# An attention and GLU block on one core: one PSUM sum for the first two head groups, its bank given to the scores, and a reshaped end

## Chip, cores, metric

The kernel runs on one core of a Trainium2 chip. The metric is the device time of one execution in microseconds (us), the median of several executions.

## The reference

One transformer block on 2048 tokens of width 640, in bf16: 32 heads of 20 columns, then a gated feed-forward part of width 1728 without a non-linearity.

```python
def reference(A_x, A_wqkv, A_wo, B_x, B_w_gate, B_w_up, B_w_down):
    def _A_ref(x, wqkv, wo):            # x: 1 x 2048 x 640, 32 heads of Dh = 20
        ...                             # q, k, v from x @ wqkv
        scores = jnp.einsum("bhqd,bhkd->bhqk", q, k) * (Dh ** -0.5)
        p = _softmax(scores, axis=-1)
        o = jnp.einsum("bhqk,bhkd->bhqd", p, v)
        return o...reshape(B, S, D) @ wo
    def _B_ref(x, w_gate, w_up, w_down):
        return ((x @ w_gate) * (x @ w_up)) @ w_down      # einsums in the original
    h = x + _A_ref(_layernorm(x), A_wqkv, A_wo)
    return h + _B_ref(_layernorm(h), B_w_gate, B_w_up, B_w_down)
```

## The kernel before

Names that the text uses. The queries are cut into six pieces p of 512, 512, 384, 256, 256 and 128; heads come in eight groups g of four. A *bank* is one 128 x 512 tile of scores (keys by queries); there are 2048, and the text tells the position in the kernel by them. Scores of a burst go to A0 or A1 in PSUM; ScalarE turns a burst into E = exp(scores) in one instruction; some banks go to VectorE instead, which computes the exponential with int16 arithmetic ("i", "fr", "hl", "ED" tiles). TensorE multiplies E with V into the bank `acc` (the row of ones in V gives the softmax sum as well). Everything else of TensorE (projections, Wo, gate, up, down) is *background work* in the banks `m`, and a scheduler in the build decides the order of all instructions from estimated durations: the order is fixed when the kernel runs. Once attention is over, the score banks become five more banks `b` for background work.

PSUM and the first two groups, which alternate by chunk of keys while K and V are still being made:

```python
acc = psum.tile([P, QW], F32, name="acc", tag="acc")
mb = tiles(psum, 2, [P, QW], F32, "m")
A = [None, pools[0].tile([P, 2, QW], F32, name="A1", tag="A1")]
A[0] = early.tile([P, 2, QW], F32, name="A0", tag="A0")
acc2 = early.tile([P, QW], F32, name="acc2", tag="acc2")   # the sum of group 1
...
# later, when group 1 is summed (about bank 128): early.release(), A0 gets 3 banks
order = [[(g, 4 * c + i) for c in range(NCH) for g in range(2) for i in range(4)]] + order[2:]
```

Every background matmul with 128 output rows is issued as four, each with its own weight load:

```python
def columns(ps, lhsT, rhs, start, stop, n, width=P):
    for i in range((width + 31) // 32):
        w = min(32, width - 32 * i)
        mm(ps[32 * i:32 * i + w, 0:n], lhsT[:, 32 * i:32 * i + w], rhs, start, stop)
```

The quotients of a finished group, with three DMAs to spread the reciprocals over the partitions:

```python
def normalise(p, g, ev):
    free = en.add("DVE", ..., tensor_copy(a[:, 0:w], bank[:, 0:w]))
    e = dma(s_ <- a[DH:P:32, 0:w])                 # the sums, to 32 partitions a head
    e = en.add("DVE", ..., reciprocal(r_, s_))
    e = dma(d <- r_)                               # to DRAM
    e = dma(b <- d, each row to 32 partitions)
    e = en.add("DVE", ..., tensor_tensor(OnT[g], a, b, ALU.mult))
```

The first loads and who waits for them:

```python
e_qk0 = [None, load_w(D, D + 160)]
e_qk0[0] = load_w(0, 160)
...
ws = ([e_k, e_qk0[1]] if b == 1 else [e_q, e_qk0[0]]) if g == 1 else [e_qk0[b]]
```

The softmax here doesn't subtract the row's maximum and nothing guards it: scores larger than these inputs give would overflow.

Of the kernel before, what the change touches and what calls it, by code (L numbers as in the profile page):

```python
# [41 lines left out]
PADR = 12  # L42
WIDTHS = [512, 512, 384, 256, 256, 128]
LASTP = len(WIDTHS) - 1
TURNED = 0
RES = 5

# [141 lines left out]
class Pe:  # L189
# [54 lines left out]
    def bg_act(self, g):  # L244
        def act(s):
            dur, fn, deps = g.steps[g.at]
            deps = list(deps)
            if g.bank is None:
                self.groups.remove(g)
                self.opens.append(g)  # L250
                deps += g.deps
                g.bank = min((b for b in self.mbanks if b.free.t is not None), key=lambda b: b.free.t)
                deps.append(g.bank.free)
                g.bank.free = Ev()
            last = g.at == len(g.steps) - 1
            self.charge(s, dur, "C", dur * 2.4, deps, [g.ev] if last else [])
            fn(g.bank.ap, g.at == 0, g.at == len(g.steps) - 1)
            g.at += 1
            if last:
                self.opens.remove(g)  # L260
                g.bank.free = g.evac(g.bank.ap, g.ev)
        return act

    def next(self):
# [4 lines left out]
        if t < INF and (kind == 2 or s > t + 100.0):  # L269
            if known([self.zeros]) <= t and sum(w for x, w in self.recent if x > t - TICK) < ENOUGH:  # L270
                need = FILL + SWITCH + (SWITCH if self.mode != "C" else 0.0)
# [5 lines left out]
    def fill(self, s):  # L277
# [3 lines left out]
        if new:  # L281
            b = next((b for b in self.mbanks if b.free.t is not None and b.free.t <= s), None)
            if b is None:
                b = Bank(self.att.acc_of(1, 0))
                b.free = self.att.acc_free[0]
            bank, deps = b.ap, deps + [b.free]
        n = bank.shape[1]
        self.charge(s, n / 2.4 + 3.0, "C", float(n), deps, [])
# [39 lines left out]
SPREAD = 1.2  # L328
# [3 lines left out]
LAG = 100  # L332
# [3 lines left out]
def kernel(  # L336
# [27 lines left out]

    pools = [tc.alloc_tile_pool(name="second", bufs=1, space=PSUM)]
    A = [None, pools[0].tile([P, 2, QW], F32, name="A1", tag="A1")]
    early = tc.alloc_tile_pool(name="early", bufs=1, space=PSUM)
    A[0] = early.tile([P, 2, QW], F32, name="A0", tag="A0")
    acc2 = early.tile([P, QW], F32, name="acc2", tag="acc2")
    late = []  # L370

    def single_banks():
# [3 lines left out]
        late[0].release()  # L376
# [11 lines left out]
    kap4 = keep.tile([P, HP], F32, name="kap4")  # L388
    kT = tiles(keep, G, [P, S], BF16, "kT")
# [11 lines left out]
    r7s = tiles(keep, 2, [P, HP], F32, "r7_")  # L401
    o7s = tiles(keep, 2, [P, P], BF16, "o7_")
# [28 lines left out]
    def columns(ps, lhsT, rhs, start, stop, n, width=P):  # L431

        for i in range((width + 31) // 32):
# [31 lines left out]
    class Att:  # L465
        def __init__(self):
# [5 lines left out]
            for p, w in enumerate(WIDTHS):  # L472
                nb = NT * w // QW
                order = [[(g, kg) for kg in range(nb)] for g in range(G)]
                if p == 0:
                    order = [[(g, 4 * c + i) for c in range(NCH) for g in range(2) for i in range(4)]] + order[2:]
# [10 lines left out]
            self.sums = {key: v // HP for key, v in self.left.items()}  # L487
# [9 lines left out]
            self.unit = 0  # L497
            self.a_free = [Ev(0.0), Ev(0.0)]
# [6 lines left out]
            self.acc_free = [Ev(0.0), Ev(0.0)]  # L505
# [67 lines left out]
        def wants_d(self):  # L573
# [8 lines left out]
            return load < D_LOAD  # L582
# [36 lines left out]
        def summing(self):  # L619
# [3 lines left out]
            for s in self.pv_left:  # L623
                p, g, _ = self.slots[s]
                if (p, g) in self.begun and not self.transposed(p, g):
                    return self.acc_of(p, g)[:, 0:WIDTHS[p]]
            return None

        def between(self, t):
# [3 lines left out]
            p, g, _ = self.slots[self.pv_left[0]]  # L633
            return (p, g) not in self.begun and self.acc_free[0].t is not None and self.acc_free[0].t <= t

        def transposed(self, p, g):
            return p == LASTP and g >= G - TURNED

        def acc_of(self, p, g):
            return acc2[:] if (p, g) == (0, 1) else acc[:]  # L640

        def s_option(self, t):
# [5 lines left out]
            at = max(t, self.a_free[u].t)  # L648
            size = 3 - u
            if u == 0 and not late and (self.acc_free[1].t is None or self.pv_at == 0 or self.acc_free[1].t > at):  # L650
                size = 2
# [6 lines left out]
        def s_act(self, u, banks):  # L658
            def act(s):
                size = len(banks)  # L660
                if size == 3 and not late:
                    early.release()
                    late.append(tc.alloc_tile_pool(name="late", bufs=1, space=PSUM))
                    A[0] = late[0].tile([P, 3, QW], F32, name="A0", tag="A0")
# [3 lines left out]
                if self.wants_d():  # L668
                    fr = [b for b in pe.mbanks if b.free.t is not None and b.free.t <= s]
                    ok = fr and self.late() <= LAG  # L670
# [130 lines left out]
        def pv_option(self, t):  # L801
# [3 lines left out]
            for s in self.pv_left:  # L805
# [8 lines left out]
                if (p, g) not in self.begun:  # L814
# [3 lines left out]
                    deps.append(self.acc_free[1 if (p, g) == (0, 1) else 0])  # L818
                rt = max(t, known(deps))
                if rt < best[0]:  # L820
                    turned = self.transposed(p, g)
                    dur = len(todo) * HP * 66.0 if turned else sum(pe_ns(n) for _, _, n, _ in todo)
                    best = rt, self.pv_act(s, es, todo, deps, dur, turned), dur, "D" if turned else "C"
# [4 lines left out]
        def pv_act(self, s, es, todo, deps, dur, turned):  # L828
            p, g, kg = self.slots[s]
            a = 1 if (p, g) == (0, 1) else 0  # L830

            def act(start):
                pe.charge(start, dur, "D" if turned else "C", 0.0 if turned else dur * 2.4, deps, [self.pv_ev[s]])
                bank = self.acc_of(p, g)
                self.sums[p, g] -= 1
                first = (p, g) not in self.begun
                self.begun.add((p, g))
                for i, (k, q, n, c) in enumerate(todo):

                    opens = first and i == 0  # L840
                    ends = self.sums[p, g] == 0 and i == len(todo) - 1
                    for j in range(HP):
                        h = g * HP + j
                        if turned:
                            mm(bank[:, VS * j:VS * j + VS], es[j][0][:, c:c + n], Vx[:, k, h * VS:h * VS + VS], opens and j == 0, ends and j == HP - 1)
                        else:
                            mm(bank[32 * j:32 * j + 32, q:q + n], Vx[:, k, h * VS:h * VS + 32],
                               es[j][0][:, c:c + n], opens, ends)
# [3 lines left out]
                if self.sums[p, g] == 0:  # L852
                    if turned:
                        self.acc_free[a] = last_quotients(g, self.pv_ev[s])
                    else:
                        self.acc_free[a] = normalise(p, g, self.pv_ev[s])
                if not self.pv_left:
# [7 lines left out]
    def filler(bank, new):  # L865
        for i in range(HP):
            mm(bank[32 * i:32 * i + 32, :], zt[:, 0:32], zt[:, 0:bank.shape[1]], new, new)
# [13 lines left out]

    def normalise(p, g, ev):
# [11 lines left out]
        bank = att.acc_of(p, g)  # L894
        free = en.add("DVE", dve_ns(w), [ev] + was,
                      lambda: nc.vector.tensor_copy(a[:, 0:w], bank[:, 0:w]), 0.5)
# [19 lines left out]
        return free  # L916

# [21 lines left out]

    def last_quotients(g, ev):  # L940

        sums = acc[:, 0:HP * VS].rearrange("p (h e) -> p h e", e=VS)
        r7, o7 = r7s[g % 2], o7s[g % 2]
        e = en.add("DVE", 110.0, [ev], lambda: nc.vector.reciprocal(r7[:].rearrange("p (h o) -> p h o", o=1), sums[:, :, DH:VS]), 0)
        e = en.add("DVE", 150.0, [e, e_o7], lambda: nc.vector.tensor_tensor(
            o7[:].rearrange("p (h e) -> p h e", e=32)[:, :, 0:DH], sums[:, :, 0:DH],
            r7[:].rearrange("p (h o) -> p h o", o=1).to_broadcast([P, HP, DH]), ALU.mult), 0)

        def turn(ps, first, last):
            pt = ps.bitcast(BF16)  # L950
            for i in range(HP):
                nc.tensor.transpose(pt[32 * i:32 * i + 32, 0:P], o7[:, 32 * i:32 * i + 32], ident[:])

        def evac(ps, x):
            q = en.add("DVE", dve_ns(P), [x, Later(lambda: wo_done.get(LASTP - 1))], lambda: nc.vector.tensor_copy(OnT[g][:, 0:P], ps.bitcast(BF16)[:, 0:P]), 0)
            on_ev[LASTP, g] = q
            return q
        front = [x for x in pe.groups if g == G - 1 and x.tag[:2] in (f"W{LASTP}", f"t{LASTP}")]
        pe.groups = [Group([e], [(pe_ns(P), turn, [])], evac, f"O{g}")] + front + [x for x in pe.groups if x not in front]
        return e  # L960
# [41 lines left out]
    def transpose_group(src, ev, dst, done, eng, prio, tag):  # L1002
        def step(c):
            def fn(ps, first, last):
                pt = ps.bitcast(BF16)
                for i in range(4):
# [39 lines left out]
    def load_w(a, b, after=None):  # L1046
        n = (b - a) * D * 2 * (2 if b - a <= 160 else 1)
# [7 lines left out]
    e_qk0 = [None, load_w(D, D + 160)]  # L1055
    e_qk0[0] = load_w(0, 160)
# [7 lines left out]
    e_kap = en.add("DVE", 80.0, [e_kap], lambda: nc.vector.tensor_reduce(kap[:], kap4[:], mybir.AxisListType.X, ALU.add), 0)  # L1064
    e_half = en.add("POOL", 100.0, [], lambda: nc.gpsimd.memset(half[:], 0.5), 0)
    e_zt = en.add("POOL", 300.0, [], lambda: nc.gpsimd.memset(zt[:], 0.0), 0)
    pe.zeros = e_zt
    e_o7 = None
    for o7 in o7s:
        e_o7 = en.add("POOL", 100.0, [e_o7], lambda o7=o7: nc.gpsimd.memset(o7[:], 0.0), 3)  # L1070
# [4 lines left out]
    e_k = load_w(D + 160, 2 * D)  # L1075
    e_q = load_w(160, D)
# [63 lines left out]
    def proj_direct(b, g, ch, eng="DVE"):  # L1140
# [24 lines left out]
        ws = ([e_k, e_qk0[1]] if b == 1 else [e_q, e_qk0[0]]) if g == 1 else [e_qk0[b]]  # L1165
# [145 lines left out]
    def second_stage(p):  # L1311
# [17 lines left out]
        for tt in range(nt):  # L1329
# [4 lines left out]
            for hf in range(2):  # L1334
                hsl = slice(hf * HD, (hf + 1) * HD)

                def evac(ps, e, hsl=hsl, hr=hr, ex=ex, hv=hv, hf=hf):
                    r = en.add("DVE", dve_ns(HD), [e, ex], lambda: nc.vector.tensor_tensor(
                        hr[:, hsl], ps[:, 0:HD], hr[:, hsl], ALU.add), 1 if not last else 0)
# [4 lines left out]
                g = sum_group(T["wo_ev"] + [ex, Later(lambda: on_ev.get((p, G - 1 - TURNED if last else G - 1)))], mats, HD, P, evac, f"W{p}{tt}{hf}")  # L1344
# [7 lines left out]
        for a in range(0, nt, step):  # L1352
# [3 lines left out]
                             [fr.get(("ln", i % 2)) for i in idx], 1.2 if not last else 0)  # L1356
# [184 lines left out]
```

## Time and profile before

| | before |
|---|---|
| median (3 executions) | 885.79 us (883.98 to 886.77) |
| profiled span | 883.0 us |
| ScalarE's exponentials, start to start | 758 instructions, 778.9 us |
| holes between them, first to last | 38.0 us |
| end of the last exponential | 834.6 us |
| from there to the end (the *tail*) | 48.4 us |

The last four rows are counted in the trace: an exponential takes 0.427 us a bank and 51 ns an instruction when its neighbours follow at once, and a hole is what a start is later than that. Where the text says that a bank is passed, or the last exponential ends, it is the start plus this price; the last end on record is up to 0.2 us later. Time = first exponential + work + holes + tail is the sum to which everything below is put.

### The profile page before, as it was taken

What the parts mean: (1) busy time and instruction counts of PE and PEld (TensorE: products, weight loads), DVE (VectorE), ACT (ScalarE), POOL (GpSimd) and SP (SyncE); (2) the same over time, 40 slices, a digit from 0 to 9 for tenths busy, and PEclk for the clock granted to TensorE, in tenths of its full rate; (3) what the DMA queues carried; (4) which work ended last, traced back from release to release, by engine and by line L of the source; (5) the groups of instructions that cost most, each with busy time, mean ns of one, the idle gap of its engine ahead of it and who ended that gap; (6) DMA issues with size and microseconds to landing.
All of it is one profiled execution on the core that took longest, in us unless ns stands there. A gap on an engine that the chain in (4) does not pass through costs nothing. (4 is left out here: it accounts for less than half of the span.)

```text
span 883.0 us, 36981 instructions
## 1 busy us (share of the span) xinstructions
PE 832.6 (94%) x16596; PEld 367.6 (42%) x16596; DVE 754.5 (85%) x1608; ACT 804.4 (91%) x780; POOL 20.8 (2%) x32
## 2 busy tenths in 40 slices
PE   6999999999999999999999999999999999999995
PEld 2444342232334322222344433344444445565774
DVE  4654886999899999999999999989989997998652
ACT  3699989999999999999999999999999999998801
POOL 2020000000000000000000000000000000000000
PEclk9999999999999999999999999999999999999999
DMA  6131212212230233211310233161034311274100
GB/s 206 39 102 29 82 56 63 84 40 79 64 89 22 67 96 90 53 41 36 67 38 28 50 79 72 27 146 34 23 90 97 66 26 31 67 154 77 23 16 19
DMA packets 132950, 56.62 MB, mean 64 GB/s; under 512 B 103096, under 2 KB 130744, under 8 KB 132792
## 3 DMA queue, kind: packets, MB, share of 16 engines
q1 hardware_dynamic: 132792, 54.27, 24.5%
q8 instruction: 129, 2.11, 1.0%
q14 instruction: 29, 0.24, 0.1%
HBM read 45.89 MB, written 8.09 MB: 61 GB/s over the span
## 5 line engine op out<-in xcount | busy, mean ns | idle before, releaser
L740 ACT ACTIVATE E<-A 128x1536 bf16<-128x1536 f32 (+1 forms) x758 | 795.4, 1183 | 21.1 <-PE A L429 12.4
L429 PE MATMUL A<-qT,kT 32*128 32x256 bf16 (+3 forms) x3024 | 296.9, 299 | 22.8 <-ACT E L740 18.6
L429 PEld LDWEIGHTS <-kT 32*128 32x128 bf16 (+1 forms) x3768 | 101.5, 92 | 256.6 <-issue 216.0
L429 PE MATMUL acc<-E,Vx 128*32 128x256 bf16 (+3 forms) x2808 | 190.1, 304 | 4.7 <-ACT E L740 3.0
L754 DVE TENSOR_SCALAR i<-m 128x512 int16<-128x512 f32 x185 | 125.9, 684 | 11.8 <-PE m L429 10.5
L429 PEld LDWEIGHTS <-Vx 128*32 128x32 bf16 x3328 | 69.5, 95 | 102.5 <-issue 94.0
L784 DVE TENSOR_TENSOR fr<-hl,fr 128x1024 bf16<-128x1024 bf16 x157 | 107.0, 682 | 2.0
L787 DVE TENSOR_TENSOR ED<-i,fr 128x1024 int16<-128x1024 int16 x157 | 106.4, 678 | 1.3
L754 DVE TENSOR_SCALAR i<-A 128x512 int16<-128x512 f32 x128 | 87.7, 685 | 11.4 <-PE A L429 9.5
L429 PE MATMUL m<-lnT,Wr 128*32 128x512 bf16 (+7 forms) x1200 | 74.9, 347 | 2.2 <-DVE lnT L1016 0.8
L429 PE MATMUL m<-qT,kT 32*128 32x256 bf16 (+3 forms) x304 | 71.6, 297 | 0.0
L429 PE MATMUL m<-Wd,hh 128*32 128x320 bf16 (+1 forms) x1456 | 71.0, 301 | 0.2 <-DVE i L754 0.2
L429 PE MATMUL m<-ln2T,wg 128*32 128x512 bf16 (+2 forms) x980 | 70.0, 348 | 0.8 <-DVE i L754 0.8
L429 PE MATMUL m<-ln2T,wu 128*32 128x512 bf16 (+2 forms) x980 | 68.7, 348 | 1.3 <-DVE i L754 1.3
L429 PE MATMUL acc<-zt 128*32 128x512 bf16 (+3 forms) x992 | 67.2, 341 | 0.0
L781 DVE TENSOR_SCALAR hl<-fr 128x1024 bf16<-128x1024 int16 x157 | 65.4, 417 | 1.5
L778 DVE TENSOR_SCALAR fr<-i 128x1024 int16<-128x1024 int16 x157 | 64.4, 414 | 1.3
L429 PEld LDWEIGHTS <-hh 128*32 128x32 bf16 (+1 forms) x1792 | 42.9, 96 | 25.8 <-issue 16.4
L429 PE MATMUL m<-shared,On 128*32 128x320 bf16 x1024 | 49.0, 301 | 0.1
L1406 DVE TENSOR_TENSOR hh<-gs,m 128x512 bf16<-128x512 bf16 (+3 forms) x66 | 36.0, 545 | 9.4 <-PE m L429 5.0
L1395 DVE CAST gs<-m 128x512 bf16<-128x512 f32 (+5 forms) x62 | 35.1, 567 | 7.0 <-PE m L429 6.3
L429 PEld LDWEIGHTS <-Wr 128*32 128x32 bf16 (+1 forms) x1200 | 27.6, 96 | 27.2 <-issue 18.1
(71 smaller groups left out, 541.4 us busy)
## 6 DMA issues: line engine op xcount, KB each, us to landing
wg<-in_B_w_gate_dram SPq DMA_DIRECT2D x47, 160.0 KB
wu<-in_B_w_up_dram SPq DMA_DIRECT2D x47, 160.0 KB
rb<-rd SPq DMA_DIRECT2D x16, 256.0 KB
kT<-kq SPq DMA_DIRECT2D x24, 128.0 KB
kq<-stg SPq DMA_DIRECT2D x24, 120.0 KB
out_dram<-ot SPq DMA_DIRECT2D x16, 160.0 KB
shared<-in_A_x_dram SPq DMA_DIRECT2D x14, 160.0 KB
Wd<-in_B_w_down_dram SPq DMA_DIRECT2D x13, 160.0 KB
```

The costliest lines, as they stand in the source:

```text
L429: nc.tensor.matmul(out_, lhsT=lhsT, rhs=rhs, start=start, stop=stop)
L740: apart(readers, nc.scalar.activation(E[:, 0:size, :], src[:, 0:size, :], ACT.Exp, scale=LN2_ / UNIT))
L754: apart(readers, nc.vector.tensor_scalar(it[:, pos, :], bank.ap, BIAS, 0.0, ALU.add, ALU.max))
L778: nc.vector.tensor_scalar(f[:, 0:n, :], it[:, 0:n, :], 127, None, ALU.bitwise_and)
L781: nc.vector.tensor_scalar(h[:, 0:n, :], f[:, 0:n, :], QR, QK, ALU.subtract, ALU.mult)
L784: nc.vector.tensor_tensor(fb[:, 0:n, :], h[:, 0:n, :], f[:, 0:n, :], ALU.mult)
L787: nc.vector.tensor_tensor(e16[:, 0:n, :], it[:, 0:n, :], fb[:, 0:n, :], ALU.add)
L1395: r = en.add("DVE", dve_ns(w), [e, was], lambda: nc.vector.tensor_copy(gs[0:M, 0:w], ps[0:M, 0:w]), 1)
L1406: r = en.add("DVE", dve_ns(w), [e, ce, was], lambda: nc.vector.tensor_tensor(hh[0:M, 0:w], gs[0:M, 0:w], ps[0:M, 0:w], ALU.mult), 1)
```

## The change

Its intent: use the idle bank of the start for scores, and shorten the end. It has these parts.

1. Groups 0 and 1 take turns in `acc` by chunk of keys; at each turn VectorE adds the partial sum to an SBUF tile (`rb`, not yet in use). `acc2` goes, and A0 has three banks from the first burst on.
2. Order of the start: the first pieces of the Q and K weights have 172 columns, not 160, so that group 1 needs no others; V of a chunk after K of the next; the later projections sorted by the bank that needs them.
3. Once attention is done, background matmuls, transposes and fillers are full 128-column ones ("F").
4. The quotients of the last three groups: a matmul with a selector and a reciprocal of 128 columns on VectorE, in place of three DMAs.
5. Feed-forward groups are released over 1.0 or less of the next stretch, not 1.2; higher priority on VectorE for Wo and LayerNorm of the fifth piece, which those of the sixth had already.
6. VectorE may take background banks for its exponentials up to bank 1800, instead of whenever background work is not over 100 banks late.

```diff
-    early = tc.alloc_tile_pool(name="early", bufs=1, space=PSUM)
-    A[0] = early.tile([P, 2, QW], F32, name="A0", tag="A0")
-    acc2 = early.tile([P, QW], F32, name="acc2", tag="acc2")
+    A[0] = pools[0].tile([P, 3, QW], F32, name="A0", tag="A0")
-    order = [[(g, 4 * c + i) for c in range(NCH) for g in range(2) for i in range(4)]] + order[2:]
+    order = [[(g, 4 * c + i) for i in range(4)] for c in range(NCH) for g in range(2)] + order[2:]
+    def partial(g, more, ev):
+        t = rb[g][:]
+        if more:
+            part_ev[g] = en.add("DVE", ..., nc.vector.tensor_tensor(t, acc[:], t, ALU.add), 0.3)
+        else:
+            part_ev[g] = en.add("DVE", ..., nc.vector.tensor_copy(t, acc[:]), 0.3)
+        return part_ev[g]
...
+QK0 = 2 * HP * DH + PADR
-    e_qk0 = [None, load_w(D, D + 160)]
-    e_qk0[0] = load_w(0, 160)
+    e_qk0 = [None, load_w(D, D + QK0)]
+    e_qk0[0] = load_w(0, QK0)
-        ws = ([e_k, e_qk0[1]] if b == 1 else [e_q, e_qk0[0]]) if g == 1 else [e_qk0[b]]
+        ws = [e_qk0[b]]
...
+    def shape(self):
+        return "F" if self.att.done() else "C"
     def columns(ps, lhsT, rhs, start, stop, n, width=P):
+        if pe.mode == "F":
+            mm(ps[0:width, 0:n], lhsT[:, 0:width], rhs, start, stop)
+            return
...
+    FAST = {LASTP: FAST_LAST, LASTP - 1: FAST_PREV}          # 2 and 1
+        if g >= G - FAST.get(p, 0):
+            spread(p, g, free, a, b, spots)                  # selector matmul, reciprocal, multiply
+            return free
...
-SPREAD = 1.2
-LAG = 100
+SPREAD = (1.0, 1.0, 0.9, 0.8)
+LEADK = 16
+M_END = 1800
-                    ok = fr and self.late() <= LAG
+                    ok = fr and self.flat < M_END
```

Cut: the scheduler's bookkeeping, the same change of shape in transposes and fillers, the sorting of the jobs, a lower load limit for VectorE at bank 128, and the removal of an unused path for the last quotients.

## The prediction

The sum came to -7.0 + 4.2 + 0.7 - 10.5 = -12.6 us, 873 us. One of its terms is cut: an allowance of +1 us in the end for weight loads of 128x128, which no measurement gave (-3.9 - 6.7 + 1 - 0.5 = -10.1). The price of a step behind the 34.9 and 31.0 us of the end is cut too; in the trace of the kernel before, a step takes 136 ns at 320 columns, 109 at 256 and 56 at 128 (medians from start to start, after 834 us), which makes 34.0 us of the steps before without the 13 small ones.

> **What bounds the kernel now.** I read the page first, then ScalarE's timeline, then the waits of the end, then the instruction starts in the trace. The page:
> ```profile
> PE 832.6 (94%) x16596; PEld 367.6 (42%) x16596; DVE 754.5 (85%) x1608; ACT 804.4 (91%) x780; POOL 20.8 (2%) x32
> ...
> PE   6999999999999999999999999999999999999995
> ...
> ACT  3699989999999999999999999999999999998801
> ```
> Three engines look full, but in slices 3 to 38 only ACT is without slack: its idle time lies in the first three slices and in the last two. So three stages: a start in which the exponentials (E<-A) have to be fed, a long middle bound by ACT, and an end in which ACT is done and TensorE finishes the feed-forward part.
>
> The groups give the middle its price:
> ```profile
> L740 ACT ACTIVATE E<-A 128x1024 bf16<-128x1024 f32 x539 | 529.5, 1061 | 10.4 <-PE A L429 9.8 <-PE m L429 0.3
> L740 ACT ACTIVATE E<-A 128x1536 bf16<-128x1536 f32 x219 | 325.1, 1485 | 10.7 <-PE m L429 6.7 <-PE A L429 2.6 <-PE acc L429 1.1
> ```
> Durations overlap; from start to start, neighbours in the trace take 904 ns at 1024 columns and 1331 ns at 1536, so 0.427 us per score bank of 512 plus 51 ns per instruction. The chain of exponentials is 539 x 0.904 + 219 x 1.331 = 778.7 us, between 17.7 us (first) and 834.6 us (end of the last): 38 us of it are holes. Of the 2048 banks, 1735 go this way, 313 go to VectorE.
>
> The start, from ACT's timeline:
> ```profile
> 27.55 1.02 ACT L740 ACTIVATE E<-A 128x1024 bf16<-128x1024 f32 x1 [0.54 <-PE A L429]
> 29.31 0.59 ACT L1154 CAST kT<-m 128x512 bf16<-128x512 f32 x1 [0.73 <-PE m L429]
> 34.72 22.11 ACT L740 ACTIVATE E<-A 128x1024 bf16<-128x1024 f32 x24 [4.83 <-PE A L429]
> 57.42 29.48 ACT L740 ACTIVATE E<-A 128x1024 bf16<-128x1024 f32 x32 [0.59 <-PE A L429]
> 89.11 11.55 ACT L740 ACTIVATE E<-A 128x1536 bf16<-128x1536 f32 x11 [2.21 <-PE m L429]
> ```
> To be seen: single exponentials with a hole before each up to 27.55; one hole of 4.83 us after 16 banks, where K and Q of the second head group are awaited; then full speed; 2.21 us at bank 128, where the bank of acc2 is turned over to A0. Later there are 2.23 us at 122.5 and 1.36 us at 130.5.
>
> The end, TensorE's timeline:
> ```profile
> 864.40 0.40 PE L429 MATMUL b<-ln2T,qT 128*32 128x128 bf16 x14 [1.57 <-issue]
> 864.58 0.77 PE L429 MATMUL m<-ln2T,qT 128*32 128x128 bf16 x40
> ...
> 867.87 0.29 PE L429 MATMUL b<-ln2T,qT 128*32 128x128 bf16 x6 [1.51 <-issue]
> ...
> 871.36 0.35 PE L429 MATMUL b<-ln2T,kT 128*32 128x128 bf16 x12 [1.51 <-issue]
> ```
> PE stops for 1.5 us, every 3.5 us, waiting for nothing that the profile shows. Counted in the trace, the stops at 846.77, 864.40, 867.87, 871.36 and 875.11 all come at PE instruction 193 of a group of 256, 256 apart. The page's "q8 instruction: 129" transfers are of 16 KB each[...], and one runs in each of those 3.5 us. So PE starves for instructions: 256 per 3.5 us, 13.7 ns each. A step here (four 32-column matmuls with their weight loads) is 8 instructions, 109 ns, but streams for only 56 ns at 128 columns. The five stops (from matmul to matmul, less streaming) are 7.2 us.
>
> [...] No 128x128 load is in the trace; the score matmuls load 32x128 (92 ns each) and still step every 56 ns, so the load was hidden there. [...]
>
> **The change part by part.** I compared the order of the instructions in both kernels; their durations are those of the trace.
>
> *Three banks for A0 from the start.* For the first 128 banks ACT needs 57.2 us in place of 57.9: only 0.7 us. What pays is the order. The first weight piece is 172 columns in place of 160, so K and Q of group 1 are made before the scores start, and the hole of 4.8 us at bank 16 goes. The price: four steps of K before the first scores. PE is still slow there (the 512-column matmuls of 11.81 us take 427 ns a step), so I put the first exponential at 18.2, 0.5 us later, with the K copy (0.6 us) behind it. Then I looked in the new order for blocks of PE work between two score bursts longer than ACT's supply. Before, these are 5.15 us (bank 16), 1.30 (64), 2.56 (128), 2.75 (209) and 2.23 (225), and the holes were 4.94, 0.78, 2.34, 2.40 and 1.47. After, they are 3.53 (bank 30, K of chunk 1), 3.67 (63, K of chunk 2), 2.56 (128) and 2.23 (191). With the LayerNorm, transposes and copies in front I get chunk 1's first exponential at 35.5, chunk 2's at 52.3, bank 128 passed at 81.5 plus a hole of 2.3, bank 256 at 136.5. Before: 143.5. **-7.0 us.** The partial sums: 2 copies and 4 adds more on VectorE, 0.69 us each, 4 us in a stretch where it is half idle, with E buffers for 19 banks (8.5 us) in between: 0.
>
> *Middle, banks 256 to 1920.* VectorE gets 302 banks, not 313, so ACT's chain is 501 x 0.904 + 248 x 1.331 = 783.0 us, +4.3 in all: +0.2 before bank 256, +2.6 here, +1.5 after. Five blocks over 1.4 us (banks 1031 to 1519, before: one of 1.36) cost perhaps 1.6 more. **+4.2 us.**
>
> *Last 128 banks.* ACT +1.5. Before had 6.1 us of holes with 3476 PE instructions in 56.3 us; now 3572, so they stay starved there (48.9 us of fetch against 51.7 us of ACT): holes of some 5.3. **+0.7 us.**
>
> *The end.* PE work after the last score matmul, in steps: before 84 of 320 columns, 16 of 320, 118 of 256, 135 of 128, and 13 small[...]: 34.9 us. After, 40 steps of 256 are done earlier: 31.0 us. **-3.9.** Whole 128-column matmuls: 2928 PE instructions become 772, 10.6 us of fetch beside 31 us of work, so stops of 7.2 us become about 0.5: **-6.7.** A weight load of 128x128 could show in the 145 steps of 128 columns: 0 by the score matmuls[...]. The last quotients go by a matmul with the selector and a reciprocal of 128 columns, by the slope of the small ones (170 ns at 4, 242 at 16: 6 ns a column) about 0.9 us, in place of a path over three DMAs that took from 836.4 to 849.4; but that path was beside other work, so it only allows the shorter end: -0.5 for waits. Lost at the last hh: the same 1 us. **-10.1, with the wait for ln2T (0.6, now behind 56 steps of Wd) -10.5.**
>
> Sum: -7.0 + 4.2 + 0.7 - 10.5 = -12.6 us of 885.8: **873 us**, 1.4% less.
>
> **The rivals.** (1) *The three-bank bursts carry it*: the start gains 11 us or more, as its idle time suggests (ACT 5 to 6 tenths from 17.7 to 40), and total 866 or less. [...] Against: from 34.7 to 86.8 ACT was full with two-bank bursts already. (2) *Full-width matmuls pay for their weights*: if every step showed a load of 90 ns (the record's duration for 128 columns), 317 steps cost 28 us, and the time would be 890 to 895. Against: the 56 ns steps of the scores[...]. (3) *ACT takes it back*: 11 more banks on ACT and the new blocks at 1031 to 1519 and 1956 cost 8 us in place of 5, and the last stage, already starved of instructions, stretches with its added work: 880. For it: the block of 2.78 us at bank 1956. (4) *VectorE becomes the bound in the middle*: it is above 9 tenths from 200 to 700 us, but gets 20 us less work (11 banks of 1.78 us): unlikely.
>
> **Range and chances.** The end's instruction stops and the moved work are sure to 2 us or so, the start to 3, the middle to 3, the weight loads to 2: some 5 to 6 us together[...]. Range 864 to 881. 2% is 868.1: faster 0.27, same 0.70, slower (over 903.5) 0.03.
>
> **What would show it.** In the changed profile: ACT without a hole at bank 16, but with holes of 2 to 4 us near 33 and 49 us; bank 128 passed near 82 to 84 us; last exponential at about 832; no 1.5 us stop by "issue" after it; steps of 128x128 at 56 to 65 ns; PE's end 36 to 38 us after the last scores. I am wrong if the start gains under 4 or over 11 us, if full-width steps take over 80 ns at 128 columns, or if new waits appear in the middle.

## The result, and the profile after

The changed kernel takes **875.31 us** (median of four executions, 874.24 to 875.66) against 885.91 us for the kernel before on the same chip (four, 883.98 to 886.77): ratio 0.9881, 95% interval 0.9863 to 0.9900. Ratios here are the mean time of one kernel's fast runs over that of the other's of the same rounds, so not quite the ratio of the medians.

| bank passed by ScalarE, us | before | predicted difference, running | after | difference, running |
|---|---|---|---|---|
| 128 | 86.8 | -5.3 | 84.7 | -2.1 |
| 256 | 143.5 | -7.0 | 138.5 | -5.0 |
| 512 | 240.1 | | 238.5 | -1.6 |
| 1024 | 433.2 | | 433.0 | -0.2 |
| 1152 | 481.9 | | 485.1 | +3.2 |
| 1920 | 778.4 | -2.8 | 779.2 | +0.8 |
| 2048 (last exponential) | 834.6 | -2.1 | 837.4 | +2.8 |
| end of the span | 883.0 | -12.6 | 873.6 | -9.4 |

So the start gains, the middle gives all of it back, and what is left is the end: the tail falls from 48.4 to 36.2 us.

The page after, the rows that answer to those in the prediction (busy time of an engine and its share of the span; then tenths of busy time in 40 slices, and of the granted TensorE clock):

```profile
PE 828.6 (95%) x15727; PEld 366.7 (42%) x15727; DVE 741.9 (85%) x1579; ACT 808.8 (93%) x771; POOL 21.3 (2%) x33
PE   6999999989999999999999999999999999999998
ACT  4789999999999999999999999999999999998931
PEclk8899999999999999999999999999999999999999
```

ScalarE has 4, 7 and 8 tenths in the first three slices where it had 3, 6 and 9 (the hole before 55.16 us below lies in the third), and the last two have 3 and 1 where they had 0 and 1. Its groups by shape show the 4.3 us of work that it got from VectorE (501 x 0.904 + 248 x 1.331 us):

```profile
L731 ACT ACTIVATE E<-A 128x1024 bf16<-128x1024 f32 x501 | 500.2, 1072 | 9.7 <-PE A L432 8.7 <-PE acc L432 0.6
L731 ACT ACTIVATE E<-A 128x1536 bf16<-128x1536 f32 x248 | 370.1, 1492 | 10.9 <-PE A L432 9.7 <-ACT E L731 0.4
```

ScalarE's timeline of the start (start, duration, engine, line, operation, tiles, count; in brackets the idle time before and what ended it):

```profile
17.02 1.45 ACT L731 ACTIVATE E<-A 128x1536 bf16<-128x1536 f32 x1 [0.50 <-PE A L432]
...
25.30 6.88 ACT L731 ACTIVATE E<-A 128x1536 bf16<-128x1536 f32 x6 [0.69 <-PE A L432]
35.04 5.97 ACT L731 ACTIVATE E<-A 128x1536 bf16<-128x1536 f32 x5 [2.86 <-PE A L432]
42.06 9.58 ACT L731 ACTIVATE E<-A 128x1024 bf16<-128x1024 f32 x8 [1.05 <-PE A L432]
55.16 29.75 ACT L731 ACTIVATE E<-A 128x1024 bf16<-128x1024 f32 x26 [3.52 <-PE A L432]
86.17 27.04 ACT L731 ACTIVATE E<-A 128x1024 bf16<-128x1024 f32 x24 [1.26 <-PE A L432]
114.38 6.52 ACT L731 ACTIVATE E<-A 128x1024 bf16<-128x1024 f32 x7 [1.17 <-PE A L432]
```

The hole of 4.83 us at bank 16 is gone. In its place are 2.86 us before 35.04 and 3.52 us before 55.16, where K of the second and third chunk is made, as the prediction said (its working had 35.5 and 52.3 for these two starts; the second came 2.9 us later).

TensorE's timeline of the end:

```profile
848.84 2.17 PE L432 MATMUL b<-Wd,hh 128*128 128x320 bf16 x14
...
857.27 1.29 PE L432 MATMUL b<-ln2T,qT 128*128 128x128 bf16 x20
858.40 0.44 PE L432 MATMUL m<-ln2T,qT 128*128 128x128 bf16 x5
858.68 0.44 PE L432 MATMUL b<-ln2T,qT 128*128 128x128 bf16 x5
...
869.38 0.31 PE L432 MATMUL m<-Wd,hh 128*128 128x320 bf16 x1 [0.29 <-DVE hh L1421]
```

No stop by "issue" is left. Five steps of 128 columns take 0.28 us from start to start (858.40 to 858.68), 56 ns each, the same as five steps of four 32-column matmuls between the stops of the kernel before (868.23 to 868.51); the 128x128 weight loads, 98 ns each in the record, do not show. A step of 320 columns takes 136 ns (median from start to start); the 14 steps of a group take 2.11 us, as the last one, with 64-row weights, starts 0.23 us after the one before it.

### The profile page after: what moved, and what is told of

Read it like the earlier page. It is cut to its first block, busy times and chain, and to the rows that moved or that the text cites. A ratio compares the mean times of both kernels' runs of the same rounds, so it can differ in the third digit from the quotient of the medians.

```text
span 873.6 us, 35178 instructions
## 1 busy us (share of the span) xinstructions
PE 828.6 (95%) x15727; PEld 366.7 (42%) x15727; DVE 741.9 (85%) x1579; ACT 808.8 (93%) x771; POOL 21.3 (2%) x33
## 4 chain that ended last, share of the span: by engine, by line
ACT 63%; PE 26%; DVE 6%; issue 5%; DMA 0%; DVEq 0%; POOL 0%; ACTq 0%
ACT E L731 62%; PE m L432 11%; PE A L432 6%; PE acc L432 5%; PE b L432 2%; DVE i L745 2%; DVE fr L775 1%; PE m L1017 1%; DVE ED L778 1%; DVE st L989 0%; DVE fr L769 0%; DVE hl L772 0%; DVE gs L1410 0%; DMA shared<-in_A_x_dram 0%; DVE shared L1001 0%
## 5 line engine op out<-in xcount | busy, mean ns | idle before, releaser
L432 PE MATMUL A<-qT,kT 32*128 32x256 bf16 (+3 forms) x3063 | 292.7, 298 | 24.1 <-ACT E L731 21.9
L432 PEld LDWEIGHTS <-kT 32*128 32x128 bf16 (+1 forms) x3448 | 100.1, 92 | 248.2 <-issue 215.0
L745 DVE TENSOR_SCALAR i<-m 128x512 int16<-128x512 f32 x176 | 120.4, 685 | 13.5 <-PE m L432 12.5
L775 DVE TENSOR_TENSOR fr<-hl,fr 128x1024 bf16<-128x1024 bf16 x151 | 103.4, 685 | 2.0
L778 DVE TENSOR_TENSOR ED<-i,fr 128x1024 int16<-128x1024 int16 x151 | 103.0, 682 | 1.3
L432 PE MATMUL m<-Wd,hh 128*32 128x320 bf16 (+1 forms) x1498 | 79.9, 301 | 1.4 <-issue 0.9
L432 PE MATMUL m<-qT,kT 32*128 32x256 bf16 (+3 forms) x265 | 68.0, 310 | 0.0
L432 PEld LDWEIGHTS <-hh 128*32 128x32 bf16 (+2 forms) x1540 | 42.2, 96 | 28.1 <-issue 15.5
L1421 DVE TENSOR_TENSOR hh<-gs,m 128x512 bf16<-128x512 bf16 (+3 forms) x70 | 37.9, 541 | 14.0 <-PE m L432 10.1
L432 PE MATMUL m<-shared,On 128*32 128x320 bf16 x960 | 44.7, 300 | 0.7 <-DVE i L745 0.4
L432 PEld LDWEIGHTS <-Wr 128*32 128x32 bf16 (+1 forms) x1200 | 28.9, 97 | 27.0 <-issue 16.7
L1410 DVE CAST gs<-m 128x512 bf16<-128x512 f32 (+2 forms) x64 | 36.0, 562 | 4.7 <-PE m L432 4.3
```

Of the source, the lines that this page charges most:

```text
L432: nc.tensor.matmul(out_, lhsT=lhsT, rhs=rhs, start=start, stop=stop)
L745: apart(readers, nc.vector.tensor_scalar(it[:, pos, :], bank.ap, BIAS, 0.0, ALU.add, ALU.max))
L775: nc.vector.tensor_tensor(fb[:, 0:n, :], h[:, 0:n, :], f[:, 0:n, :], ALU.mult)
L778: nc.vector.tensor_tensor(e16[:, 0:n, :], it[:, 0:n, :], fb[:, 0:n, :], ALU.add)
L1410: r = en.add("DVE", dve_ns(w), [e, was], lambda: nc.vector.tensor_copy(gs[0:M, 0:w], ps[0:M, 0:w]), 1)
L1421: r = en.add("DVE", dve_ns(w), [e, ce, was], lambda: nc.vector.tensor_tensor(hh[0:M, 0:w], gs[0:M, 0:w], ps[0:M, 0:w], ALU.mult), 1)
```

## The experiments

Twelve kernels in three batches; each ratio is to the kernel before in the same rounds (11 executions of it a batch). Each batch ran on another chip, and the changed kernel was not run again in them, so it is compared with the others by ratios of different rounds. Parts 5 (the priorities) and 6 were not taken away alone. "Tail" and the banks' times are from each one's trace.

| run | median us | ratio (95%) | bank 256 | bank 512 | bank 1920 | last exp. | tail |
|---|---|---|---|---|---|---|---|
| before | 885.79 | | 143.5 | 240.1 | 778.4 | 834.6 | 48.4 |
| changed | 875.31 | 0.9881 | 138.5 | 238.5 | 779.2 | 837.4 | 36.2 |
| before_f | 881.10 | 0.9928 (0.9904 to 0.9951) | 143.7 | 240.4 | 778.6 | 837.3 | 41.4 |
| after_c | 879.85 | 0.9914 (0.9891 to 0.9936) | 137.0 | 237.0 | 777.8 | 836.6 | 41.2 |
| start_only | 885.10 | 0.9971 (0.9944 to 0.9998) | 136.4 | 236.4 | 779.6 | 834.1 | 47.7 |
| after_qk | 876.89 | 0.9876 (0.9852 to 0.9900) | 138.2 | 238.2 | 778.7 | 836.5 | 38.9 |
| f_last | 873.85 | 0.9879 (0.9847 to 0.9912) | 137.3 | 237.3 | 778.0 | 836.0 | 36.3 |
| i4 (wrong result) | 875.62 | 0.9894 (0.9858 to 0.9929) | 137.2 | 235.8 | 774.8 | 833.8 | 40.2 |
| after_jobs | 877.72 | 0.9924 (0.9893 to 0.9956) | 143.1 | 238.9 | 779.7 | 837.3 | 39.1 |
| before_f_order | 881.44 | 0.9963 (0.9933 to 0.9994) | 139.7 | 239.2 | 781.5 | 841.3 | 40.2 |
| b4 | 870.97 | 0.9843 (0.9819 to 0.9867) | 136.3 | 236.3 | 774.7 | 831.8 | 34.5 |
| b4k48 | 872.33 | 0.9853 (0.9829 to 0.9877) | 137.7 | 235.3 | 774.0 | 831.4 | 38.6 |
| after_spread | 878.07 | 0.9920 (0.9901 to 0.9939) | 136.8 | 236.8 | 780.1 | 837.6 | 38.9 |
| after_dma | 875.17 | 0.9888 (0.9868 to 0.9909) | 136.5 | 236.6 | 777.3 | 833.3 | 39.8 |

Seven of these have the changed kernel's order up to bank 512 (the changed kernel, after_c, start_only, f_last, b4, after_spread, after_dma): they pass bank 256 at 136.3 to 138.5, the changed kernel's own profile being the slowest. The record of the granted clock goes with this: from 15 us on it had half clock in two stretches of 3.4 us (at 22.0 and at 39.0 us), after_c in one (at 22.4), b4 in none; the mean granted clock of these executions was 0.991, 0.993 and 0.996. (The kernel before has no such record until 27.7 us, and its page shows 9 tenths or more from the first slice; but its 512-column background steps took 0.40 to 0.43 us until then, and 0.21 to 0.23 us later.) So up to 2 us of the start look like the luck of an execution, and totals are compared by ratios only.

### The instruction stops of the end: before_f and after_c

before_f adds part 3 alone to the kernel before:

```diff
     def columns(ps, lhsT, rhs, start, stop, n, width=P):
+        if pe.mode == "F":
+            mm(ps[0:width, 0:n], lhsT[:, 0:width], rhs, start, stop)
+            return
```

(with `shape()`, the transposes and the filler as in the change)

> The kernel before with one part of the change alone: full 128-column matmuls, transposes and fillers once attention is done. Theory (the end starves for instructions): the five stops of 7.2 us after the last exponential go, PE instructions after the last score matmul fall from 2928 to about 890, last exponential unchanged at 834.6, time from there to the end 48.4 -> 41 to 42.5; 879 us, ratio 0.992 to 0.993. Rival (the quotients' three DMAs, 836 to 849, become what sets the end): gain under 4 us, a new wait of 2 us or more for the DMA of rb in the end, 882 to 884. Rival (weight loads of 128x128 show): no gain.

after_c takes it alone away from the changed kernel:

```diff
     def shape(self):
-        return "F" if self.att.done() else "C"
+        return "C"
```

> The changed kernel without the full-width shape: 32-column matmuls to the end, all else the same (same order, last exponential at 837.4). Theory: 2569 PE instructions after the last score matmul in place of 772, at 13.7 ns each 35 us against 30 us of streaming, stops of 1.5 us by issue come back; +5 to +7 us, 880.5 to 882.5. Rival (stops before came from something that the changed order has removed as well, e.g. the DMA traffic of the quotients): +0 to +2 us, no stops.

Measured: before_f's tail is 41.4 us, 7.0 less than before's 48.4, with no stop by "issue" after the last exponential and no wait for a DMA. The total gained 0.72%, 6.4 us: inside the interval of the expected ratio, 881.1 where 879 was expected. In its profile the last 128 banks took 58.6 us where before's, with the same order, took 56.3: TensorE's idle time put down to "issue" in those banks is 4.9 us in this execution and 2.3 us in the other. after_c's tail is 41.2 us, 5.0 more than the changed kernel's, and the stops are back in its TensorE timeline:

```profile
861.85 0.46 PE L432 MATMUL m<-ln2T,qT 128*32 128x128 bf16 x20 [1.51 <-issue]
...
865.33 0.91 PE L432 MATMUL b<-ln2T,kT 128*32 128x128 bf16 x52 [1.51 <-issue]
...
869.08 0.72 PE L432 MATMUL m<-Wd,hh 128*32 128x320 bf16 x14 [1.03 <-issue]
```

They are 3.5 and 3.75 us apart, close to the 3.5 of the kernel before, and all lie at the same place of a group of 256 PE instructions. In total after_c gained 0.86% on the kernel before, where the changed kernel gained 1.19%: 2.9 us, less than the 5 to 7 expected (and the two intervals overlap), but 5.0 us in the tail. The theory holds: both directions move the stops, and neither rival (a DMA that takes over, weight loads that show) was seen.

### The start: start_only, after_qk, before_f_order, after_jobs

start_only undoes every end part of the changed kernel:

```diff
-        return "F" if self.att.done() else "C"
+        return "C"
-SPREAD = (1.0, 1.0, 0.9, 0.8)
+SPREAD = (1.2, 1.2, 1.2, 1.2)
-FAST_LAST = 2
-FAST_PREV = 1
-LNP = (1.2, 1.2, 1.2, 1.2, 0, 0)
-WP = (1, 1, 1, 1, 0, 0)
+FAST_LAST = 0
+FAST_PREV = 0
+LNP = (1.2, 1.2, 1.2, 1.2, 1.2, 0)
+WP = (1, 1, 1, 1, 1, 0)
```

> The changed kernel with every end part undone: 32-column shape, quotients of all groups by DMA, spread 1.2 and the old priorities; what stays is the start (shared sum, three banks, first weight piece, job order) and the new rule for VectorE's share. ACT gets 783.4 us of exponentials as in the changed kernel. Theory (the start's gain is given back in the middle, the net gain is the end's): bank 256 at 138 to 139, last exponential at 836 to 839, 48 us from there; 884 to 887, ratio 0.998 to 1.002. Rival (the start's 5 us survive, and it is the moved work and its blocks that cost the middle): last exponential at 830 to 832, 879 to 881.

Measured: 885.10 us, in the theory's range; the ratio, 0.9971, is just below it (the interval, 0.9944 to 0.9998, reaches in), a gain of some 2.6 us. The last exponential, 834.1, lies between the theory's 836 to 839 and the rival's 830 to 832. Bank 256 is passed 7.1 us earlier than before, bank 512 3.7 us earlier, bank 1920 1.2 us later. That is the course of the changed kernel without its end: the shared sum and the third bank, from which the change has its name, are worth some 0.3% together with the new order of the start and the new rule for VectorE's banks.

after_qk puts the old first weight piece back:

```diff
-QK0 = 2 * HP * DH + PADR
+QK0 = 2 * HP * DH
-        ws = [e_qk0[b]]
+        ws = ([e_k, e_qk0[1]] if b == 1 else [e_q, e_qk0[0]]) if g == 1 else [e_qk0[b]]
```

> The changed kernel with the first weight piece of 160 columns again, so K and Q of group 1 wait for the second pieces. Theory (the start's gain is the order of the loads, not the three banks): a hole of 5 us or more at bank 16 again, no holes of 3 us near 35 and 55, bank 256 passed 3 to 5 us later than in the changed kernel, at 141.5 to 143.5. Its schedule also gives ACT 11 banks less (778.1 us), so the last exponential is at 835 to 838 and the whole 874 to 878. Rival (three-bank bursts and the shared sum make the gain): bank 256 at 138 to 140.

The hole is back in ScalarE's timeline (the line of 33.21, the same 4.83 us as before), yet bank 256 is passed at 138.2:

```profile
33.21 21.86 ACT L731 ACTIVATE E<-A 128x1536 bf16<-128x1536 f32 x19 [4.83 <-PE A L432]
56.70 4.62 ACT L731 ACTIVATE E<-A 128x1024 bf16<-128x1024 f32 x4 [1.63 <-PE A L432]
```

My theory missed here and its rival came in. The total is that of the changed kernel (0.9876 against 0.9881). The hole at bank 16, on which the prediction put its eye, is time in which work for later holes gets done: close it, and the waits come at banks 30 and 63.

before_f_order has the new order of the start but keeps acc2 and two-bank bursts (and has the full-width end, so it compares with before_f):

```diff
+QK0 = 2 * HP * DH + PADR
-    e_qk0 = [None, load_w(D, D + 160)]
-    e_qk0[0] = load_w(0, 160)
+    e_qk0 = [None, load_w(D, D + QK0)]
+    e_qk0[0] = load_w(0, QK0)
-        ws = ([e_k, e_qk0[1]] if b == 1 else [e_q, e_qk0[0]]) if g == 1 else [e_qk0[b]]
+        ws = [e_qk0[b]]
```

(and the values and jobs in the changed kernel's order)

> The kernel before with two parts of the change: the full-width end and the order of the start (first weight piece of 172 columns, values and jobs in the new order), but with acc2, separate sums for the first two groups and two-bank bursts until bank 128. Theory (the order makes most of the start's gain, the shared sum adds little): no hole of 5 us at bank 16, bank 256 at 138 to 140 as in the changed kernel. Rival (three banks and the shared sum make it, as the run with the old first weight piece suggests, which had 138.2): bank 256 at 141 to 144. In both cases the holes of the start are under 26 us only if the order matters. In all 877 to 881.

It is ahead at bank 64 (51.1 against 56.9 us in before_f), loses 5.8 us in holes up to bank 128, and passes bank 256 at 139.7, 4.0 us ahead. So the new order without the shared sum and the three banks brings 4.0 us at bank 256, the shared sum with the new order but without the new first piece 5.3 (after_qk), and all together 6.7 (median of the seven): none of these is the cause alone. What bank 256 cannot do without, the next run shows, is the new order of V and of the later projections. In total it is not better than before_f (0.9963 against 0.9928): its tail of 40.2 is shorter, its last 128 banks (59.7 us) and its middle are longer.

after_jobs gives the changed kernel the old order of V and dense projections:

```diff
-    jobs = []
-    for T_, when in enumerate((128, 192, 320, 384)):
-        jobs.append((when - LEADK, len(jobs), proj_dense(0, T_, 0)))
-        ...
-    for when, _, g in sorted(jobs, key=lambda x: x[:2]):
-        due([g], when)
+    vq = [(t, 1) for t in range(NT)] + [(t, 2) for t in range(NT)]
+    for T_, when in enumerate((128, 192, 320, 384)):
+        due([proj_dense(0, T_, 0)], when)
+        for ch in range(NCH):
+            due([proj_dense(1, T_, ch)], when + 16 * ch)
+            due([proj_v(*vq.pop(0)) for _ in range(4) if vq], when + 16 * ch + 16)
```

(and V of a chunk before K of the next)

> The changed kernel with the kernel-before's order of the V and dense K/Q projections. Theory (the start's gain after bank 256 was lent: that order moves VectorE work behind bank 128, and VectorE takes 8 banks fewer by bank 512): ACT's work falls from 783.0 to 778.3 us, bank 256 is passed 2 to 4 us later (139.5 to 142) by blocks of 4.38, 3.16 and 2.16 us at 192 to 242, and at bank 512 the kernel is level with the changed one or ahead (236 to 239); 872 to 876 in all. Rival (the order of the jobs is what makes the start): bank 512 at 240 or later, 877 to 880.

Bank 256 came at 143.1, later than expected (139.5 to 142) and only 0.4 us ahead of the kernel before, by the three holes from the blocks that its order shows:

```profile
115.39 5.12 ACT L731 ACTIVATE E<-A 128x1024 bf16<-128x1024 f32 x5 [3.67 <-PE A L432]
123.19 12.88 ACT L731 ACTIVATE E<-A 128x1024 bf16<-128x1024 f32 x12 [2.69 <-PE A L432]
137.63 7.87 ACT L731 ACTIVATE E<-A 128x1024 bf16<-128x1024 f32 x7 [1.56 <-PE A L432]
```

But at bank 512 it is at 238.9, nearly level with the 236.3 to 238.5 of the seven: of the 5 to 7 us that it was behind at bank 256, 4.2 are made up in the next 256 banks. The stretch from bank 256 to 512 takes 96.6 us before, 95.8 in after_jobs and 100.0 or 100.1 in all seven. Counted up to bank 512, VectorE takes 63 banks before, 63 in after_jobs and 55 in the changed kernel; eight banks at 0.427 us are 3.4 us of ScalarE, and its work up to there is indeed 201.9 us before and 205.3 in the changed kernel. This is where the gain of the start goes. It is not the partial sums, which after_jobs has as well: the order that gets ScalarE through the start sooner leaves VectorE with copies to make where it took banks before (between banks 256 and 512 it makes 25 copies to stg and Vx, 15.0 us, in the changed kernel; 17 copies, 10.5 and 10.3 us, before and in after_jobs). The total of after_jobs (0.9924) is behind the changed kernel's all the same (the intervals just overlap); the expected 872 to 876 was missed by 2 us.

### The middle: i4, b4, b4k48

Between banks 1024 and 1152 the changed kernel has 4.1 us of holes, before 0.8. The largest is in ScalarE's timeline:

```profile
435.83 31.19 ACT L731 ACTIVATE E<-A 128x1536 bf16<-128x1536 f32 x30 [0.71 <-PE A L432]
469.20 11.55 ACT L731 ACTIVATE E<-A 128x1536 bf16<-128x1536 f32 x10 [2.18 <-PE A L432]
```

Before it TensorE does a block of Wo (m<-shared,On), which the prediction took for the cause. The timeline of all engines there offers another cause:

```profile
466.44 2.35 PE L432 MATMUL m<-shared,On 128*32 128x320 bf16 x64
466.54 0.42 DVE L769 TENSOR_SCALAR fr<-i 128x1024 int16<-128x1024 int16 x1
466.88 0.69 DVE L778 TENSOR_TENSOR ED<-i,fr 128x1024 int16<-128x1024 int16 x1
467.48 0.48 DVE L1353 TENSOR_TENSOR h<-m,h 128x320 bf16<-128x320 f32 x1
467.88 0.68 DVE L745 TENSOR_SCALAR i<-A 128x512 int16<-128x512 f32 x1
...
468.71 0.60 PE L432 MATMUL A<-qT,kT 32*128 32x384 bf16 x10
```

The third bank of A0 had been given to VectorE. VectorE reads it only at 467.88 to 468.56, after it has finished an older pair (ED) and a sum of Wo, and the next scores for A0 start at 468.71. The block of Wo ends within 0.1 us of that too, so the trace alone does not decide. If VectorE's int16 buffers (three pairs) are what makes it late, a fourth takes the hole away.

i4:

```diff
-NI16 = 3
+NI16 = 4
-    stg = tiles(p1, 2, [P, QW], BF16, "stg")
+    stg = [t[:, 0:QW] for t in l2]
```

> The changed kernel with four int16 buffers for VectorE's exponentials in place of three (the space: the staging tiles share the memory of the second LayerNorm's). Its order has none of the PE blocks at banks 1031 to 1519 and 1956. Theory (the hole of 2.39 us at 469 is A0's third bank held until VectorE, out of int16 buffers, has read it, and the block of Wo only fills the wait): banks 1024 to 1152 lose 3 us of holes (4.1 to under 1.2), bank 1920 passed at 775 to 777 in place of 777.8 to 779.2; but 33.8 us of streaming are left after the last scores in place of 30.9, so 872.5 to 876 in all. Rival (Wo at the head of the queue makes the hole): 3 us or more of holes stay between 1024 and 1152.

Its result was wrong (relative error 0.096): the staging tiles and those of the second LayerNorm are in use at the same time, so the memory that I gave it was not free. Its times stand, as it does the same operations: the holes between banks 1024 and 1152 are 1.5 us in place of 4.1, bank 1920 is passed at 774.8. It leaves more work for the tail (40.2), so the total is no better.

b4 has the fourth buffer where memory is free, from about bank 520 on:

```diff
+        k = att.ipos % len(I16t)
+        I16t.append(pool.tile([P, 2, QW], I16, name="i16_3", tag="i16_3"))
+        att.i_free.append(Ev(0.0))
+        att.ipos = k
         p2["wd_ev"] = []
```

> The changed kernel with a fourth int16 buffer for VectorE's exponentials from about bank 520 on (in the memory that the projections free), meant to be right where the earlier trial was not. Order the same until then; blocks at 1031 to 1519 and 1956 gone, new ones of 2.5 us at 1562 and 1.4 us at 1947. ACT 783.5 us, 29.2 us of streaming left after the last scores (30.9 in the changed kernel). Theory (VectorE short of buffers makes the holes of the middle): holes between banks 1024 and 1152 under 1.5 us in place of 4.1, and the gain stays: 2 to 4 us less in all, 870.5 to 873, ratio 0.983 to 0.986. Rival: the holes move to the block at 1562 and the total stays within 1 us of the changed kernel.

The result is right, and b4 is the fastest kernel here, 870.97 us, ratio 0.9843. ScalarE's timeline has one line through the place of the hole:

```profile
444.18 41.39 ACT L731 ACTIVATE E<-A 128x1024 bf16<-128x1024 f32 x38
```

Holes between 1024 and 1152 are 1.1 us, bank 1920 is passed at 774.7 (777.3 to 779.2 in the four kernels with the changed kernel's order up to there). Part of this is the luck of the start: from bank 256 to 1920 it takes 638.4 us, they 640.7 to 640.8. In total b4 is ahead of the changed kernel by 0.38%, of different rounds, and the intervals touch. The tail is 34.5 us, since its order leaves 29.2 us of streaming after the last scores, not 30.9. The theory held against its rival: the hole goes with the buffer. That the block of Wo only filled a wait which the scheduler expected is the likely reading, not shown by itself.

b4k48 adds an earlier due date for the jobs of the start:

```diff
-LEADK = 16
+LEADK = 48
```

> As the one before it, with the jobs of the start (dense K/Q and V) due 48 banks earlier in place of 16, so that their VectorE copies are spread over banks 128 to 256 where it had slack: ACT 779.5 us in place of 783.0, no block over 1.3 us after bank 223, 32.4 us of streaming after the last scores. Theory (the start's gain was handed to VectorE's share): last exponential at 829 to 833, the tail 38 us; 867 to 871, ratio 0.979 to 0.983, the best of all. Rival (what is taken from ACT comes back as holes or as tail): 872 to 875.

ScalarE's work fell to 779.7 us as its order said, but the last exponential came at 831.4, as in b4 (831.8), and the tail was 38.6 us: 0.9853, not distinguishable from b4. What was taken from ScalarE came back as holes (35.6 us in place of 30.9) and tail. The expected 867 to 871 was missed by over a microsecond; the rival came in.

### The last 128 banks: f_last

```diff
-        if pe.mode == "F":
+        if pe.mode == "F" or att.flat >= 1920:
             mm(ps[0:width, 0:n], lhsT[:, 0:width], rhs, start, stop)
```

(the same in the transposes; the order is that of the changed kernel)

> The changed kernel, same order, but the background matmuls and transposes are issued full-width already from bank 1920 on, so the last 128 banks have 2440 PE instructions in place of 3570. Theory (PE is starved of instructions there: 3570 at 13.7 ns are 48.9 us beside 51.7 us of ACT): banks 1920 to 2048 take 54 to 55.5 us in place of 58.1, no stop by issue over 0.5 us there, the tail of 36 us unchanged; 871 to 873 us, ratio 0.983 to 0.986. Rival (the holes there are order, bursts against background work[...]): 57.5 us or more for these banks, 875 or slower.

My theory failed. With 2440 PE instructions in place of 3570 no instruction stop over 0.15 us is left in the trace, and yet banks 1920 to 2048 take 57.9 us (58.1 in the changed kernel), and the holes are the same ones. The first fence is the changed kernel's ScalarE timeline, the second f_last's:

```profile
793.70 1.02 ACT L731 ACTIVATE E<-A 128x1024 bf16<-128x1024 f32 x1 [0.59 <-PE acc L432]
795.34 11.13 ACT L731 ACTIVATE E<-A 128x1536 bf16<-128x1536 f32 x11 [0.62 <-PE A L432]
```

```profile
793.05 1.02 ACT L731 ACTIVATE E<-A 128x1024 bf16<-128x1024 f32 x1 [0.69 <-PE acc L432]
794.93 10.32 ACT L731 ACTIVATE E<-A 128x1536 bf16<-128x1536 f32 x10 [0.85 <-PE A L432]
```

So in this order of the work the stops for instructions do not make these holes; that the order makes them is what is left, and not shown further. For the order of the kernel before this is not settled: there the last 128 banks took 2.3 us longer in the execution with 2.6 us more of stops (before_f).

### Moved work and the quotients: after_spread, after_dma

```diff
-SPREAD = (1.0, 1.0, 0.9, 0.8)
+SPREAD = (1.2, 1.2, 1.2, 1.2)
```

> The changed kernel with the feed-forward groups spread over 1.2 of the next stretch again in place of 1.0 or less: 70 steps of 256 columns of the gate and up weights are left for after the last score matmul in place of 48. Theory (the moved work is worth what it streams): tail 2 to 2.4 us longer than the 36.2 of the changed kernel, 38 to 39; last exponential 836 to 838 (ACT 783.4), total 876 to 879. Rival (work moved ahead of the last scores only stretches the last banks): last exponential 2 us earlier, total as the changed kernel.

Tail 38.9 us, last exponential 837.6, 878.07 us: all three as expected. By the ratio the earlier release is worth 0.39%, 3.5 us (0.9920 against 0.9881, of different rounds); 2.7 us of it are seen in the tail. The middle gains too: from bank 256 to 1920 after_spread takes 643.3 us and start_only, with the same spread, 643.3, where the four with the changed spread take 640.7 to 640.8.

```diff
-FAST_LAST = 2
-FAST_PREV = 1
+FAST_LAST = 0
+FAST_PREV = 0
```

> The changed kernel with the last three quotients by three DMAs each again. Its order leaves 31 more steps of 256 columns for after the last scores (34.3 us of streaming in place of 30.9). Theory (the DMA path is hidden beside work, the spread only allows a shorter end): tail 39.5 to 41 us, with no wait over 1 us for the quotients, total 878 to 880. Rival (the path of some 13 us from the last sum to the quotient is what the end waits for): PE idle 2 us or more before the Wo steps, tail 42 us or more, 881 or more.

The tail is 39.8 us, as expected, and its longest wait in TensorE's timeline is 0.59 us, for ln2T and not for a quotient. But the total, 875.17 us, misses the expected 878 to 880, and its ratio, 0.9888, is that of the changed kernel: the last 128 banks took 56.0 us in place of 58.1 and have no hole between 775 and 810 us. The selector matmuls let Wo of the fifth piece run at about bank 1956, ahead of the last scores; the changed kernel's holes from 791 to 807 us lie beside and behind that block, and ScalarE loses there much of what the tail gains.

## Why the prediction was right, and where its terms were not

The total, 873, is 2.3 us from the measured 875.31, and within the range. That it is so close is partly luck: in the profiles the start, the middle and the last banks came out 2.0, 1.6 and 1.1 us worse than their terms and the end 1.7 us better. Of its signs, the hole at bank 16, the stops by "issue" and the 56 ns steps came as said; the last exponential came at 837.4, not 832, and TensorE's end 34.0 us after the start of the last scores, not 36 to 38. One of its signs of being wrong came as well: new waits in the middle.

**Start, -7.0.** The changed kernel's profile has -5.0, the seven profiles of the same order -5.0 to -7.2 against 143.5, with a median of -6.7. The step was right in size. Its parts were not: bank 128 came at 82.5 to 84.7, not at 81.5, and the stretch from 128 to 256 gained 3 us where the prediction had 1.7. "What pays is the order" is half true: with the old first weight piece, and so with the hole at bank 16, five of these microseconds stay; with the old order of the later projections next to nothing stays at bank 256 (143.1).

**Middle, +4.2.** Measured +5.8 from bank 256 to 1920 (634.9 before, 640.7 in the changed kernel, 640.7 to 640.8 in the three others with its order). ScalarE's added work, predicted at 2.6, is 2.4. The holes, predicted at 1.6, are 3.4 (16.7 in place of 13.3). This term was mis-sized, and its cause misread: the blocks stood where it said (holes of 0.83, 2.39 and 1.01 us at banks 1031, 1114 and 1514, from start to start), but because VectorE was short of int16 buffers. With the fourth buffer these holes are gone. The term also left out what the earlier release does here: without it the middle would have lost 8.4 us (after_spread).

**Last 128 banks, +0.7.** Measured +1.8: 1.5 of work as predicted, and holes of 6.5 in place of the 5.3. "So they stay starved there" was the wrong step, at least for the order after: f_last takes the starvation away and nothing is gained.

**End, -10.5.** Measured -12.2. Of it, from the tails: the instruction stops 5.0 us given the rest of the change (after_c) and 7.0 alone (before_f), predicted 6.7; the earlier release 2.7 (after_spread) and the quotients 3.6 (after_dma), predicted 3.9 and 0.5, together 6.3 against 4.4. The weight loads of 128x128 cost nothing that shows: 56 ns a step of 128 columns, beside loads of 98 ns in the record. The moved work and the quotients are partly paid for in the last 128 banks, so the sum over both stages is -12.2 + 1.8 = -10.4, where the prediction had -9.8.

**The rivals.** The three-bank bursts did not carry it. Full-width matmuls paid nothing for their weights (56 ns a step of 128 columns and 136 of 320, in both shapes). ScalarE took back 7.6 us (5.8 and 1.8), nearly the 8 of the third rival; the total stayed under its 880 because the last stage did not stretch beyond that and the end gained more than forecast. VectorE did become a bound in one sense that the fourth rival did not have: not by its busy time, which fell, but by its buffers.

Three slips in the working changed little: -10.1 and the wait of 0.6 make -10.7, not -10.5; the second rival's 28 us would have made some 900, not 890 to 895; and the first of the five stops comes four groups of 256 instructions before the second, not one.

What stays open: why the stops for instructions between banks 1920 and 2048 differ by 2.6 us between two executions with the same order, what the priorities and the new rule for VectorE's banks are worth, and how much of start_only's 0.3% is real.

## What to carry to other kernels

Where two engines share a stream of work that is balanced between them, an idle gap closed early is not a gain until the end is reached: follow the running difference at fixed points of the work, since the partner may take over less. A block of other work before a late instruction can be what the engine did while it waited; look for the release of the buffer (here the third bank of A0, read late by VectorE) before moving the block, and give the buffer first. Where the trace shows an engine stopping by "issue" (here TensorE, for 0.80 to 1.57 us at a time, at the same place of a group of 256 instructions), fewer and larger instructions are worth measuring alone: here 5 to 7 us of the tail, 2.9 to 6.4 us of the total, for a change of shape whose cost did not show.
